# Sliding-window attention and gated convolution FFN: three V loads on ScalarE's DMA queue, with new order lists

## The chip, the core and the metric

The kernel runs on one core of a Trainium2 chip. The core has five engines that work side by side: TensorE (PE) for matmuls, VectorE (DVE), ScalarE (ACT) and GpSimd (POOL) for everything element by element, and SyncE (SP), which here only issues DMAs. ScalarE can issue DMAs too, on a queue of its own. Each engine runs its instructions strictly in order; between engines, semaphores make an instruction wait for what it needs. The metric is the device time of one execution in microseconds (us); the time of a kernel is the median of several runs.

## What is computed

For 8 sequences of 576 positions, 8 heads of 64: attention in which position i sees only positions within 32 of it, then a gated FFN with a convolution of three taps along the sequence.

```
scores = (q @ k^T) / 8, only where |i - j| <= 32
x      = softmax(scores) @ v          # heads side by side: 512 wide
h      = relu(x @ w_in)               # 512 -> 1024
c[s]   = w0*h[s-1] + w1*h[s] + w2*h[s+1]   # per channel
out    = (h * sigmoid(c)) @ w_out     # 1024 -> 512
```

Inputs and output are float32; the kernel computes matmuls in bf16.

## The kernel before

**Attention** is done by sequence b (0 to 7) and half s (0 or 1). For each half, `load_qk` (L502) loads q and k in two pieces each, one for heads 0 to 3 and one for heads 4 to 7, 288 KB a piece, in runs of 2304 bytes. `load_v` (L534) loads V in chunks of 128 positions that are shifted by 32 (chunk 0 has 96 rows, chunk 4 has 96); its runs are 256 bytes, since a row of one head is 64 floats. For sequence 0, chunk 2 is split into rows 0 to 64, which belong to half 0, and rows 64 to 128, which belong to half 1. `cast_qk` (L514) turns q and k to bf16; `cast_v` (L544) makes the bf16 tile ve of V, and `shift_v` (L553) a second one, vo, which holds V shifted by 64 positions. `transposes` (L591) brings q and k to head-dimension-major form through PE, and a copy from PSUM by ACT or DVE writes qT or kT. `scores` (L635) multiplies them and takes exp on ACT (L683); the window is kept either by a matmul that adds a band of large negative numbers, or by a multiplication with a mask on POOL or DVE (L690). `values` (L693) multiplies with V on PE (L711), takes the reciprocal of the sums (L729) and writes the normalised rows xn on DVE (L731). `turn` (L738) transposes xn into xT: with PE for sequences 0 and 1, and by a DMA transpose on SP's queue (L744) for the others.

**The FFN** works on 12 chunks of 384 positions; chunks 0 and 1 are cut into two pieces each. For each of 8 blocks m of 128 hidden channels, `hidden` (L811) multiplies with w_in (L856), takes relu on ACT into hT (L876), applies the three taps in one of five ways (PE with diagonal matrices L931, ACT L939, DVE L944, or all three taps on POOL, L919 and L924), takes tanh on ACT (L954; the gate is written with tanh), and gates on DVE (L971). `project` (L985) multiplies with w_out (L996), copies from PSUM to y, and stores (L1014, the last chunk L1010).

**Weights.** w_in and w_out come in two halves of 1 MB each through the same two staging tiles wst (L576) and are cast block by block; w_in's casts may be on ACT, POOL or DVE, w_out's are on POOL. The 24 diagonal matrices of the taps (L489 on ACT, L491 on DVE) are made from `conv_w`, which ACT's queue loads (L475) and PE transposes (L478).

**Order.** Each of these steps is an operation with a number. Nothing is planned while the program is built: `ORDER` lists all operation numbers in program order, `PICK` names the engine for those that have a choice, `CHOICE` the way in which each block's taps or each window mask is done, `BANKS` the PSUM bank for each use. `Plan.place` walks through ORDER and gives each operation a start by its own cost figures; the start only sorts the operations of all engines into one program and says where `warm` puts idle matmuls (L1023) that keep PE busy in the head. So within one engine or queue, program order is the order of these lists. Every load but conv_w is on SP's queue. A load into a staging tile waits there until its former content has been cast, and all that stands behind it in the queue waits too.

Of the kernel before, what the change touches and what calls it, by code (L numbers as in the profile page):

```python
# [17 lines left out]
    0, 0, 0, 0, 1, 0, 0, 2, 0, 0, 4, 4, 4, 4, 3, 2, 4, 4, 4, 4, 0, 4, 4, 4, 2, 4, 0, 2, 0, 0, 0, 4,  # L18
    4, 4, 4, 4, 4, 4, 4, 4, 4, 4, 0, 4, 2, 1, 1, 2, 2, 0, 2, 0, 2, 4, 3, 4, 4, 2, 2, 2, 1, 2, 1, 2,
    3, 0, 3, 2, 2, 2, 2, 2, 0, 2, 2, 3, 0, 1, 2, 2, 4, 0, 0, 2, 1, 2, 4, 2, 2, 2, 2, 3, 2, 3, 2, 0,  # L20
    2, 0, 2, 2, 2, 2, 1, 1, 0, 2, 2, 3, 2, 1, 4, 2, 2, 0, 3, 2, 2, 0, 2, 0, 2, 2, 2, 2, 4, 3, 3, 2,
    3, 3, 2, 2, 2, 2, 2, 2, 2, 2, 2, 3, 2, 2, 3, 3, 2, 2, 3, 2, 3, 2, 3, 2,
# [11 lines left out]
    67, 74, 0, 29, 36, 30, 27, 34, 37, 51, 1, 47, 2, 22, 12, 21, 48, 52, 28, 35, 45, 49, 50, 46, 55,  # L34
    53, 26, 25, 7, 68, 75, 89, 85, 86, 4, 56, 32, 33, 70, 69, 43, 76, 77, 44, 91, 87, 18, 54, 8, 31,
    42, 24, 38, 92, 14, 11, 88, 72, 83, 41, 39, 57, 58, 5, 60, 61, 90, 95, 59, 62, 63, 64, 65, 66,
    97, 17, 96, 82, 93, 117, 121, 225, 98, 120, 99, 118, 219, 119, 221, 223, 112, 114, 213, 6, 94,
    226, 113, 16, 211, 116, 40, 115, 71, 81, 217, 215, 78, 79, 220, 222, 73, 224, 80, 84, 100, 214,
    212, 103, 251, 216, 13, 133, 140, 9, 3, 19, 218, 227, 132, 139, 236, 101, 10, 23, 252, 102, 104,
    105, 233, 228, 229, 110, 106, 20, 108, 253, 243, 107, 111, 152, 148, 230, 109, 262, 244, 245,  # L40
    246, 153, 247, 15, 231, 232, 237, 263, 382, 234, 383, 384, 239, 240, 135, 134, 142, 141, 150,
    385, 238, 241, 388, 154, 151, 248, 149, 242, 155, 249, 250, 235, 258, 259, 268, 264, 265, 269,
    389, 158, 159, 171, 177, 156, 157, 256, 254, 386, 387, 376, 276, 378, 255, 260, 377, 286, 257,
    277, 402, 374, 379, 287, 288, 261, 278, 403, 283, 380, 170, 176, 136, 172, 178, 122, 125, 126,
    123, 143, 270, 279, 173, 179, 396, 375, 381, 271, 124, 137, 280, 294, 404, 397, 284, 272, 398,
    188, 190, 266, 186, 184, 285, 295, 296, 393, 411, 281, 191, 282, 273, 185, 394, 189, 187, 395,
    274, 405, 406, 267, 407, 412, 390, 399, 275, 400, 408, 391, 413, 401, 392, 409, 197, 198, 146,
    410, 138, 144, 147, 127, 130, 195, 163, 160, 161, 162, 164, 131, 196, 192, 193, 129, 128, 461,
    462, 306, 307, 312, 165, 166, 168, 169, 305, 304, 311, 320, 321, 174, 145, 318, 319, 194, 297,
    298, 289, 290, 322, 167, 418, 414, 415, 323, 324, 416, 291, 325, 426, 422, 182, 342, 341, 180,  # L50
    346, 353, 357, 417, 433, 420, 175, 183, 292, 423, 427, 293, 354, 358, 419, 181, 436, 421, 437,
    328, 438, 434, 435, 202, 308, 313, 339, 340, 345, 329, 326, 199, 351, 203, 204, 439, 327, 355,
    430, 352, 440, 200, 201, 431, 441, 442, 432, 330, 301, 302, 309, 316, 356, 363, 364, 359, 360,
    310, 317, 314, 331, 332, 334, 209, 210, 428, 429, 361, 333, 335, 336, 451, 456, 207, 452, 453,
    424, 315, 468, 343, 349, 469, 475, 443, 205, 362, 299, 425, 486, 457, 446, 447, 448, 458, 471,
    470, 476, 344, 348, 454, 206, 455, 208, 487, 459, 449, 488, 489, 444, 544, 545, 482, 540, 541,
    484, 485, 300, 445, 450, 350, 347, 368, 460, 483, 365, 366, 369, 370, 367, 506, 507, 511, 522,
    523, 493, 494, 504, 505, 510, 546, 547, 518, 519, 520, 516, 542, 543, 568, 556, 521, 517, 564,
    569, 490, 491, 473, 478, 557, 570, 526, 527, 558, 492, 495, 565, 566, 567, 463, 464, 559, 560,
    550, 551, 548, 549, 528, 554, 555, 529, 530, 472, 480, 474, 477, 481, 499, 500, 496, 497, 501,  # L60
    524, 552, 656, 657, 663, 371, 338, 508, 514, 512, 571, 584, 525, 498, 585, 586, 561, 674, 553,
    572, 562, 573, 563, 574, 575, 587, 588, 509, 579, 580, 576, 581, 670, 671, 465, 466, 692, 337,
    372, 596, 597, 675, 479, 513, 515, 531, 532, 534, 535, 533, 582, 577, 583, 536, 598, 599, 602,
    603, 608, 617, 627, 600, 604, 578, 628, 618, 695, 694, 699, 706, 693, 658, 698, 659, 664, 609,
    708, 709, 610, 601, 622, 605, 707, 611, 672, 673, 589, 619, 629, 623, 620, 621, 630, 631, 644,
    645, 624, 710, 711, 640, 641, 632, 633, 676, 677, 606, 607, 642, 612, 591, 636, 788, 373, 613,
    614, 660, 303, 590, 625, 615, 704, 592, 705, 643, 646, 647, 616, 637, 638, 626, 593, 594, 648,
    634, 635, 639, 715, 716, 503, 789, 795, 502, 729, 730, 661, 666, 790, 737, 738, 802, 803, 806,
    807, 681, 745, 718, 682, 763, 719, 741, 742, 733, 734, 678, 679, 764, 746, 765, 683, 717, 680,
    668, 665, 747, 766, 767, 712, 735, 773, 697, 791, 796, 804, 649, 713, 736, 805, 662, 669, 687,  # L70
    688, 774, 689, 739, 684, 685, 686, 539, 537, 467, 650, 740, 768, 769, 748, 749, 538, 696, 870,
    871, 731, 755, 756, 757, 732, 743, 750, 759, 653, 775, 776, 744, 760, 770, 667, 771, 864, 751,
    777, 702, 758, 772, 752, 654, 703, 793, 792, 778, 860, 865, 808, 884, 861, 885, 761, 714, 762,
    809, 753, 754, 779, 651, 652, 700, 701, 720, 899, 800, 812, 798, 797, 866, 862, 813, 721, 780,
    886, 887, 722, 888, 723, 983, 794, 801, 817, 724, 867, 863, 872, 818, 725, 879, 819, 880, 980,
    981, 987, 873, 889, 890, 874, 875, 868, 869, 894, 876, 810, 811, 900, 827, 831, 881, 895, 882,
    903, 896, 897, 877, 691, 690, 824, 982, 823, 883, 904, 785, 783, 595, 786, 891, 892, 784, 905,
    906, 901, 878, 893, 898, 907, 908, 909, 988, 781, 782, 910, 1000, 1001, 814, 815, 816, 994, 995,
    996, 997, 822, 727, 828, 726, 919, 998, 902, 999, 911, 920, 921, 922, 834, 835, 935, 936, 1005,
    1002, 826, 830, 825, 829, 940, 838, 839, 1006, 1003, 931, 932, 937, 938, 836, 925, 941, 837,  # L80
    939, 832, 926, 840, 923, 927, 841, 942, 943, 929, 924, 949, 848, 928, 950, 944, 945, 946, 845,
    912, 930, 849, 799, 958, 951, 952, 846, 1112, 985, 990, 933, 842, 914, 833, 1016, 850, 1111,
    1017, 655, 728, 1018, 821, 959, 913, 947, 948, 953, 954, 843, 934, 963, 915, 968, 1007, 820,
    1057, 1118, 1129, 1130, 844, 1022, 1059, 955, 956, 960, 961, 964, 1053, 1054, 1060, 1058, 969,
    965, 966, 1004, 916, 917, 1125, 1065, 847, 984, 992, 851, 970, 962, 971, 967, 957, 986, 993,
    989, 1008, 1066, 1032, 1126, 1083, 1033, 972, 1084, 852, 1009, 853, 1055, 1056, 1078, 1019,
    1023, 1034, 1113, 787, 1021, 1035, 1069, 1070, 1073, 1028, 1029, 1010, 1085, 1079, 1080, 1011,
    1081, 1030, 1031, 1012, 1013, 1074, 1082, 1075, 973, 974, 1071, 1072, 1025, 1063, 1064, 1038,
    854, 855, 1061, 1076, 1077, 856, 1091, 1092, 1093, 1062, 1039, 1086, 1087, 975, 976, 991, 1094,
    1114, 1020, 1026, 1115, 1041, 1042, 1119, 1127, 1131, 1132, 1128, 1088, 1089, 1120, 1043, 1040,  # L90
    977, 978, 1136, 1137, 1133, 1067, 1096, 1068, 1036, 1116, 1027, 1121, 1024, 1123, 1090, 1095,
    1138, 1097, 1047, 1048, 1049, 1134, 1037, 1135, 1147, 1148, 1153, 1149, 1163, 1150, 1154, 1100,
    1098, 1099, 1164, 857, 859, 858, 1183, 1189, 1190, 1184, 1044, 1045, 1214, 1193, 1194, 1191,
    1192, 1159, 1160, 1165, 1195, 1196, 1161, 1162, 1046, 1215, 1166, 1216, 1117, 1124, 1142, 1143,
    1144, 1152, 1156, 1101, 1102, 1222, 1103, 1217, 1218, 1223, 1226, 1139, 1140, 1141, 1185, 1187,
    1186, 1204, 1205, 1199, 1188, 1197, 1198, 1104, 1209, 1015, 918, 1014, 1105, 1200, 1206, 1210,
    1224, 1211, 1225, 1122, 1050, 1051, 1244, 1245, 1227, 1230, 1207, 1219, 1248, 1212, 1231, 1232,
    1220, 1249, 1221, 1233, 1108, 1109, 1201, 1202, 1213, 1203, 1234, 1106, 1169, 1271, 1228, 1229,
# [206 lines left out]
def kernel(  # L305
# [84 lines left out]
    def pe(n, count=1):  # L390
        return ("PE", count * (n / 2400.0 + 0.003))
# [708 lines left out]
```

## Time and profile before

| | |
|---|---|
| median of 7 runs | 220.13 us (219.85 to 220.47) |
| the profiled execution | 219.31 us |
| its span (first to last instruction) | 217.6 us |
| TensorE clock granted | 0.997 |
| busy: PE, DVE, ACT, POOL | 199.0, 194.0, 189.0, 180.3 us |
| DMA traffic | 45.92 MB, nearly all on one queue |

The span is what the profile shows; the profiled execution's own time is 1.71 us longer. In the profile's rows a line number is a line of the kernel; L400, L402 and L406 are the helper `copy` on ACT, POOL and DVE, so that one has to read the names of the tiles: st for q and k as loaded (qst, kst), nat as cast (qn, kn), vst, ve, vo, wst. "SPq" and "ACTq" are the issues of DMAs. In brackets stands how long the engine had been idle and what ended it.

### The profile page before, as it was taken

How to read it: one execution, taken by the hardware profiler on the slowest of the kernel's cores; microseconds unless marked ns; L12 is line 12 of the kernel's file. 1: busy time of each engine (PE TensorE's matmuls, PEld its weight loads, DVE VectorE, ACT ScalarE, POOL GpSimd, SP SyncE). 2: the span in 40 equal slices, each digit the busy share in tenths (PEclk: the TensorE clock that was granted, in tenths of full speed). 3: DMA queues.
4: the chain of work that ended last, by engine and by line, in shares of the span. 5: the costliest groups of instructions: out<-in, count | busy, mean ns of one | idle time of the engine just before them, and what ended most of it. 6: DMA issues, size and time to landing. Idle time of an engine off the chain costs nothing.

```text
span 217.6 us, 6442 instructions
## 1 busy us (share of the span) xinstructions
PE 199.0 (91%) x2445; PEld 124.8 (57%) x2462; DVE 194.0 (89%) x391; ACT 189.0 (87%) x406; POOL 180.3 (83%) x225
## 2 busy tenths in 40 slices
PE   2577789998999989999999999999999999999993
PEld 0454668967777566656555475456566455455441
DVE  5468996769899899999999999999999999999962
ACT  3198999976798999999998999799999999999860
POOL 3352999999886866999999999999999999999940
PEclk9999999999999999999999999999999999999998
DMA  5999999998993599999899999998399531170074
GB/s 170 261 275 347 333 326 274 350 266 182 314 232 98 78 222 306 220 282 229 165 216 270 212 293 262 285 257 228 84 137 217 110 145 26 39 275 18 0 281 154
DMA packets 68675, 45.92 MB, mean 211 GB/s; under 512 B 53644, under 2 KB 53924, under 8 KB 68644
## 3 DMA queue, kind: packets, MB, share of 16 engines
q1 hardware_dynamic: 68608, 45.49, 83.8%
q8 instruction: 19, 0.31, 0.7%
q14 instruction: 12, 0.10, 0.2%
q10 hardware_dynamic: 36, 0.01, 0.0%
HBM read 32.52 MB, written 9.44 MB: 193 GB/s over the span
## 4 chain that ended last, share of the span: by engine, by line
POOL 39%; PE 25%; DVE 14%; ACT 7%; DMA 7%; issue 5%; SPq 1%; POOLq 1%; DVEq 0%
POOL tmp L924 13%; POOL tmp L919 12%; PE ps_all L996 8%; PE ps_all L856 6%; POOL vo L402 6%; POOL ve L402 4%; PE ps_all L608 3%; DMA xT<-xn 2%; DMA vst<-in_v_dram 2%; POOL kn L402 2%; DMA kst<-in_k_dram 2%; DVE xn L731 2%; ACT ps_all L954 2%; PE ps_all L931 2%; ACT attn L683 2%
## 5 line engine op out<-in xcount | busy, mean ns | idle before, releaser
L856 PE MATMUL ps_all<-xT,w_in_sb 128*128 128x385 bf16 (+4 forms) x448 | 73.6, 305 | 2.4 <-DVE w_in_sb L406 1.3
L944 DVE SCALAR_TENSOR_TENSOR ps_all<-hT,conv_w_sb,ps_all 128x384 f32<-128x384 bf16 (+3 forms) x117 | 65.6, 594 | 3.7 <-PE ps_all L931 2.0
L996 PE MATMUL ps_all<-w_out_sb,gT 128*128 128x512 bf16 (+1 forms) x279 | 66.1, 373 | 2.0 <-DVE y L406 0.5
L971 DVE SCALAR_TENSOR_TENSOR gT<-ps_all,hT 128x384 bf16<-128x384 f32 (+3 forms) x112 | 51.5, 492 | 3.5 <-ACT ps_all L954 2.9
L856 PEld LDWEIGHTS <-w_in_sb 128*128 128x128 bf16 x448 | 40.0, 98 | 23.7 <-issue 2.5
L876 ACT ACTIVATE hT<-ps_all 128x385 bf16<-128x385 f32 (+4 forms) x112 | 48.5, 466 | 3.6 <-PE ps_all L856 3.3
L996 PEld LDWEIGHTS <-gT 128*128 128x128 bf16 x296 | 28.1, 98 | 31.0 <-issue 1.8
L683 ACT ACTIVATE attn<-ps_all 128x1024 bf16<-128x1024 f32 (+1 forms) x40 | 37.1, 951 | 3.4 <-PE ps_all L668 3.3
L924 POOL TENSOR_TENSOR tmp<-tmp 128x384 f32<-128x384 f32 (+1 forms) x38 | 37.3, 982 | 3.2
L954 ACT ACTIVATE ps_all<-ps_all 128x384 f32<-128x384 f32 (+3 forms) x93 | 38.6, 449 | 0.2
L402 POOL TENSOR_SCALAR vo<-vst 64x1024 bf16<-64x1024 f32 (+1 forms) x32 | 33.3, 1041 | 6.1 <-DMA vst<-in_v_dram 3.7
L919 POOL TENSOR_SCALAR tmp<-hT,conv_w_sb 128x384 f32<-128x384 bf16 (+1 forms) x57 | 34.4, 610 | 3.8 <-ACT hT L876 2.1
L939 ACT ACTIVATE ps_all<-hT,conv_w_sb 128x384 f32<-128x384 bf16 (+3 forms) x49 | 28.2, 582 | 2.5 <-DVE gT L971 1.8
L731 DVE TENSOR_TENSOR xn<-ps_all,rec 128x512 bf16<-128x512 f32 (+1 forms) x32 | 25.6, 817 | 0.5
L402 POOL TENSOR_SCALAR ve<-vst 128x512 bf16<-128x512 f32 (+1 forms) x38 | 24.3, 648 | 1.4
L402 POOL TENSOR_SCALAR qn<-qst 128x1152 bf16<-128x1152 f32 (+1 forms) x19 | 19.2, 1017 | 6.6 <-DMA qst<-in_q_dram 5.8
L400 ACT COPY y<-ps_all 128x512 f32<-128x512 f32 (+1 forms) x28 | 16.3, 590 | 5.3 <-PE ps_all L996 5.3
L402 POOL TENSOR_SCALAR kn<-kst 128x1152 bf16<-128x1152 f32 (+1 forms) x17 | 17.6, 1036 | 2.8 <-DMA kst<-in_k_dram 2.7
L608 PE MATMUL ps_all<-ident,kn 128*128 128x128 bf16 x144 | 13.1, 224 | 6.0 <-DVE kn L406 5.9
L931 PE MATMUL ps_all<-hT,diag_w 128*128 128x192 bf16 (+3 forms) x113 | 17.1, 271 | 0.0
L711 PE MATMUL ps_all<-ve,attn 128*64 128x65 bf16 x384 | 15.2, 197 | 1.5 <-DVE ve L406 0.6
L400 ACT COPY kT<-ps_all 128x640 bf16<-128x640 bf16 (+1 forms) x21 | 15.7, 755 | 0.9 <-PE ps_all L668 0.7
(66 smaller groups left out, 238.4 us busy)
## 6 DMA issues: line engine op xcount, KB each, us to landing
qst<-in_q_dram SPq DMA_DIRECT2D x32, 288.0 KB, 5.4
kst<-in_k_dram SPq DMA_DIRECT2D x32, 288.0 KB, 5.8
out_dram<-y SPq DMA_DIRECT2D x11, 768.0 KB, 5.7
vst<-in_v_dram SPq DMA_DIRECT2D x23, 256.0 KB, 5.0
vst<-in_v_dram SPq DMA_DIRECT2D x16, 192.0 KB, 5.3
wst<-in_moe_w_in_dram SPq DMA_DIRECT2D x2, 1024.0 KB, 8.8
wst<-in_moe_w_out_dram SPq DMA_DIRECT2D x2, 1024.0 KB, 8.2
out_dram<-y SPq DMA_DIRECT2D x2, 256.0 KB, 2.0
```

What stands on the lines that cost most here:

```text
L400: nc.scalar.copy(out=out_, in_=in_)
L402: nc.gpsimd.tensor_scalar(out=out_, in0=in_, scalar1=1.0, scalar2=0.0, op0=ALU.mult, op1=ALU.add)
L683: add(act(2 * w), t + 0.1, lambda e: nc.scalar.activation(at, ps(sl, 0, 1024).rearrange("p (e x) -> p e x", e=2)[:, :, 0:w], AF.Exp, bias= ...
L731: add(dve(4 * n * D), t + 0.1, lambda e: nc.vector.tensor_tensor(out=xn[i].rearrange("p c (e g) d -> p (c e) g d", e=2)[:, 2 * cs[0]:2 * ( ...
L856: nc.tensor.matmul(ps(sl, 512 * y, 512 * y + n), w_in_sb[:, kc, m * 128:(m + 1) * 128], x_[:, kc, a0:a1], start=(kc == 0), stop=(kc == KC ...
L876: nc.scalar.activation(o_, i_, AF.Relu, bias=0.0, scale=0.5)
L919: nc.gpsimd.tensor_scalar(out=tv(not own), in0=hview(m, o0, o1, kk - 1), scalar1=conv_w_sb[:, kk, m:m + 1], scalar2=0.0, op0=ALU.mult, op1 ...
L924: nc.gpsimd.tensor_tensor(out=tv(0), in0=tv(0), in1=tv(1), op=ALU.add)
L944: add("DVE", tt + 0.1, lambda e, m=m, y=y, n_=n_, pv=pv, ks=by_dve: nc.vector.scalar_tensor_tensor(out=pv(y), in0=hview(m, o0, o1, ks[n_] ...
L954: nc.scalar.activation(o_, i_, AF.Tanh, bias=0.0, scale=1.0)
L971: nc.vector.scalar_tensor_tensor(out=o_, in0=i_, scalar=1.0, in1=hview(m0, o0, o1, 0, w), op0=ALU.add, op1=ALU.mult,)
L996: nc.tensor.matmul(ps(sl, f0, f1), gT[ig][:, m, 128 * i:128 * i + 128], w_out_sb[:, m, f0:f1], start=(m == 0), stop=(m == MB - 1),)
```

## The change

Three loads of V for sequence 0, half 0 (chunk 0, chunk 1, and rows 0 to 64 of chunk 2: 192, 256 and 128 KB) are issued by ScalarE instead of SyncE:

```diff
+    def queue(second):
+        return (("ACTQ", 0.6), nc.scalar) if second else (sp(), nc.sync)
...
     def load_v(b, c, p0, p1, prio, rel):
         s0 = 128 * c - PAD + p0
-        add(sp(0.57), prio, lambda e: nc.sync.dma_start(
+        on, q_ = queue(b == 0 and p0 < 64 and c < 3)
+        add(on, prio, lambda e: q_.dma_start(
             vst[p0:p1, c, :, :], v[b, :, s0:s0 + p1 - p0, :].rearrange("h p d -> p h d")
...
-        on = dict([act(n), pool(n), both(n)]) if b == 0 else pool(n)
+        on = dict([act(n), pool(n), ("DVE", n / 960.0 + 0.14)]) if b == 0 else pool(n)
```

The last pair is in `cast_qk` and, like the other numbers that the diff changes in `load_qk`, `load_v`, `load_w` and `conv_weights` (cost figures and a mode), it only feeds the figures of `Plan.place`. `CHOICE`, `ORDER`, `PICK` and `BANKS` are new in whole. Read as lists by engine, these are the differences that the prediction speaks of:

| | before | after |
|---|---|---|
| SP's queue, first issues | q half 1 (1 piece), k half 0 (2), q half 0 (2), q half 1 (1), V chunk 1, V chunk 2 rows 0 to 64, k half 1 (2), V chunk 0, V chunk 3, w_in (2), V chunk 2 rows 64 to 128, V chunk 4, then sequence 1 | k half 0 (2), q half 0 (2), q half 1 (1), k half 1 (2), q half 1 (1), w_in (2), V chunk 4, V chunk 2 rows 64 to 128, V chunk 3, then sequence 1 |
| ACT's queue | conv_w | conv_w, V chunks 0, 1, 2 rows 0 to 64 |
| PE, first | k transposes, conv_w between them, q, scores | conv_w, k transposes, q, scores |
| DVE, first | q cast, k cast, conv_w copy, 2 diagonals, kT copy, qT copy | conv_w copy, 4 diagonals, V casts 0 and 1, a V shift, 2 kT copies, qT copy |
| PE, half 0 of sequence 0 | scores, half 1's transposes, both values | scores, values, transposes, values, transposes |
| first w_in block used (7) is cast by | DVE, behind 2 xT copies | POOL |
| SP's queue, transposes of sequence 2 | two, then V of sequence 3 (chunks 3, 4) and a q load, two more, then the k loads of sequence 4 | four, with V's chunk 3 ahead, and chunk 4 and the k loads behind |

| operations | before | after |
|---|---|---|
| q/k casts on ACT, DVE, POOL | 1, 3, 36 | 2, 1, 37 |
| V casts on ACT, DVE, POOL | 2, 1, 38 | 0, 2, 39 |
| V shifts on ACT, DVE, POOL | 1, 3, 32 | 1, 5, 30 |
| w_in and w_out casts on ACT, DVE, POOL | 2, 4, 10 | 2, 3, 11 |
| diagonals on ACT, DVE | 15, 9 | 11, 13 |
| y copies on ACT, DVE | 28, 9 | 30, 7 |
| window by band, POOL mask, DVE mask | 20, 4, 16 | 19, 5, 16 |
| blocks with all taps on POOL | 19 | 19 |

## The prediction

> **What bounds the kernel now.** I read the page's chain first, then busy time by stage, then the first 23 us in order of time, then the DMA view.
>
> ```profile
> POOL 39%; PE 25%; DVE 14%; ACT 7%; DMA 7%; issue 5%; SPq 1%; POOLq 1%; DVEq 0%
> ```
>
> No engine owns the end; the chain changes hands. Stage by stage (columns: length, then busy us of PE, PEld, DVE, ACT, POOL, granted clock, DMA share, GB/s):
>
> ```profile
> 0.00:22.80 22.80, 13.11 (x176) 8.20 (x176) 14.92 (x44) 13.54 (x25) 9.05 (x21) 1.00 0.96 262
> 22.80:46.00 23.20, 21.97 (x368) 19.03 (x370) 19.13 (x46) 21.78 (x66) 22.18 (x33) 1.00 1.07 316
> 66.90:99.00 32.10, 31.36 (x430) 19.64 (x432) 31.02 (x59) 30.80 (x62) 26.78 (x33) 1.00 1.01 198
> 99.00:140.00 41.00, 40.39 (x467) 23.40 (x470) 40.22 (x73) 38.36 (x75) 39.20 (x41) 1.00 1.02 238
> ```
>
> From 22.8 us on all four engines are nearly full (in 99 to 140: DVE idle 0.8 of 41, POOL 1.8). Only the head is loose: PE idles 9.7 of 22.8 us, DVE 7.9, POOL 13.8, while the DMA engines are 96% busy. The head is bound by data, the rest by total work. A change of load order can win in the head; afterwards only moved work or changed stalls count.
>
> The first 23 us in order of time (start, length, ..., idle before and its releaser):
>
> ```profile
> 8.96 0.67 POOL L402 TENSOR_SCALAR qn<-qst 128x576 bf16<-128x576 f32 x1 [0.53 <-DMA qst<-in_q_dram]
> 11.66 0.62 POOL L402 TENSOR_SCALAR vo<-vst 64x512 bf16<-64x512 f32 x1 [1.09 <-DMA vst<-in_v_dram]
> 14.03 1.02 ACT L683 ACTIVATE attn<-ps_all 128x1024 bf16<-128x1024 f32 x1
> 15.07 0.62 POOL L402 TENSOR_SCALAR vo<-vst 64x512 bf16<-64x512 f32 x1 [0.51 <-DMA vst<-in_v_dram]
> 17.08 0.19 PE L711 MATMUL ps_all<-ve,attn 128*64 128x65 bf16 x1 [0.60 <-DVE ve L406]
> 18.59 0.62 POOL L402 TENSOR_SCALAR w_in_sb<-wst 128x512 bf16<-128x512 f32 x1 [1.94 <-DMA wst<-in_moe_w_in_dram]
> 22.83 3.67 PE L856 MATMUL ps_all<-xT,w_in_sb 128*128 128x256 bf16 x32 [1.33 <-DVE w_in_sb L406]
> ```
>
> The second half of q of half sequence 0 landed at 8.96, V's chunk 1 at 11.66, V's chunk 0 at 15.07, the first half of w_in at 18.59. The second exp was done at 15.05, but the rest of P times V went at 17.08: V's late chunks and their casts cost 2.0 us. The first hidden matmul (L856) starts at 22.83. V is slow to move: from 12 to 15.2 us mostly V, from 15.2 to 16.5 w_in:
>
> ```profile
> DMA packets 1957, 0.77 MB, mean 240 GB/s; under 512 B 1811, under 2 KB 1811, under 8 KB 1957
> DMA packets 256, 0.51 MB, mean 393 GB/s; under 512 B 7, under 2 KB 7, under 8 KB 256
> ```
>
> **Part 1, three V issues go to ScalarE's queue.** They take 192, 256 and 128 KB off SP's queue. SP's issue rows are 0.65 us each and V's chunk 1, issued at 4.71, landed 7 us later, so SP's issue time wasn't the limit: leaving SP is worth 0 by itself, what counts is the order. On ACT they cost 3 x 0.60 (the row of the one ACT issue) = 1.8 us: 0.8 to 3.2 with the conv issue, then the table load (1.28) to 4.5. ACT's first work before began at 4.75 after 2.04 of idle: hidden; without that cover, 1.8. If the issue of V waits for the zeroing of the V tile (DVE, 1.62 to 2.73), it starts up to 1.3 late, behind it only the other V issues, the table load and ACT's first scalings.
>
> Here the Trainium skill speaks against the change: "DMA: Bandwidth & Descriptors", section "Issuing engines are not separate DMA queues", says that issues from several engines run on the same 16 DMA engines and interleave, so only the initiation time is saved. The row: 96% DMA busy already with one queue. By the rule q pays for V's bytes; without it q would land at 8.96 as before and the first hidden matmul about 1.0 earlier than I reckon. I follow the rule. By then 1152 KB of q and k and 576 KB of V must have come: six q/k transfers, the same 1728 KB, had landed by 9.9; V's 0.59 MB at 220 to 240 instead of 270 GB/s adds 0.4. So the last of q is at **10.3** (bounds: 9.0 if q keeps its rate, 12.5 if the mix runs at the 170 GB/s of the page's first slice).
>
> **Part 2, the chain of the first half.** q at 10.3 instead of 8.96 is 1.3 late; its two casts now run on ACT and POOL side by side instead of one after the other on POOL, -0.3: scores, exps **1.0 late**, second exp done at 16.05. V has long landed, so its 2.0 us wait goes: P times V at 16.1 to 16.5, reciprocal 0.2, xn 0.65 (group 2 is normalised before, behind the first exp): xn done at 17.5 instead of 19.77. Then, on DVE, a qT copy 0.82, xT 0.65, a w_in cast 0.8, xT 0.65: 20.4. Before it was two xT and a w_in cast, 3.06 with gaps. With 0.6 for the matmul's own wait L856 starts at **21.0 instead of 22.83: -1.8**. On DVE the V casts and one shift (0.6 + 0.6 + 0.7) now stand in front of the two kT copies: if V's chunk 2 is late, kT is late.
>
> **Part 3, w_in ahead of the second half's V.** 256 KB less of V lies before it; at 240 GB/s that is 1.1: w_in lands at 17.5, its second half 1.1 earlier as well. Chunks 3, 4 and the rest of 2 land behind w_in, with the same 5.5 MB in all as before; ACT cast chunk 4 at 25.07 without waiting, so that they are hidden behind the first hidden chunk, with some 2 us of cover; beyond that each us is one for the second half's P times V.
>
> So the lead at 23 us is between 1.1 (w_in's second half, the later data) and 1.8; I carry **-1.5**.
>
> **Part 4, the new lists.** Counting the operations that the lists put on each engine, and pricing differences with their rows: *ACT* four diagonal scalings less (-1.4), two V casts less (-1.2), two y copies more (+1.2), two 384-wide L939 less and four narrow ones for one (-0.1), copies +0.4: -1.1. *DVE* two q/k casts less (-1.5), a w_in cast less (-0.8), two y copies less (-1.4), two wide and two 255-wide taps less for two narrow (-1.4), four diagonals more (+1.4), one V cast and two shifts more (+1.9), the rest +0.7: -1.1. *PE* tap matmuls +0.8, mask adds -0.1: +0.7. *POOL* a q/k cast, a V cast and a w_in cast more (+2.0), a 512-wide mask more (+1.15), two shifts less (-1.2), a tap block of 129 for one of 255 (-0.9): +1.0. From 99 us on the chain is POOL's, but POOL idles 5.3 us in 66.9 to 99, so most is covered; uncovered it is 1.0. I take **+0.3**. The tail keeps its shape (0).
>
> A stall that could move: SP's queue at the transposes of sequence 2.
>
> ```profile
> 70.41 2.60 SPq L744 DMA_TRANSPOSE xT<-xn  x2
> 73.11 2.13 SPq L536 DMA_DIRECT2D vst<-in_v_dram  x2
> 75.33 0.57 SPq L505 DMA_DIRECT2D qst<-in_q_dram  x1
> 75.97 2.58 SPq L744 DMA_TRANSPOSE xT<-xn  x2
> ```
>
> Two transposes held SP for 6.1 us (its longest wait), and loads of V and k queue behind them; POOL then idles 1.8 and 1.2 for them. In the new order four transposes stand together, with V's chunk 4 and the k loads of sequence 4 behind. Bounds: -3 (POOL's 5.3 idle shrinks) to +3 (k lands after POOL asks for it, near 80 us); value 0, since V's chunk 3 of sequence 3, for which POOL waited 1.8, now goes out ahead of the group, while the k loads now go behind two more transposes.
>
> **Sum.** 219.31 (span 217.60 and 1.71 around it) - 1.5 + 0.3 = 218.1 in the profile's terms; the median of the runs is 0.82 above the profiled one, so **218.9**.
>
> **The rivals.**
> *A, the lead is lost by 99 us.* For: the same bytes in all, POOL without idle from 21 to 65, and POOL sets the second half. Against: PE and DVE carried the chain from 20 to 66, and POOL waited 2.1 us at 66.9 for hT. Time: no lead left, the added POOL work covered by its idle time: 220.1.
> *B, slower: the first half's q, or V's chunk 2 ahead of kT on DVE, comes too late.* The page's section "Queues, rings and completion order" has each DMA engine take whole packets from its queues in turn; no row here has two busy queues. q and k move in runs of 2304 bytes, V in runs of 256, so turns could share time in a way that holds V back. For: 240 GB/s where V moves, and DVE runs in order. Against: V needs only a third of the bytes. It decides at 10.3 + 1.8 = 12.1 us: a landing later than that takes the whole gain. At 13.5 it is +1.4, with +0.3 of work less what overlaps: 221.2.
> *C, the stall at the transposes shrinks too* by about 2 of its 3: 216.9.
>
> **Numbers.** Likeliest case 0.45, its own range 218.0 to 219.6; A 0.17; B 0.20; C 0.18. A change within 0.2% (0.44 us) is about what a measurement of this kernel can't tell from none. Faster: 0.43 + 0.18 + 0.05 of A = 0.66. Same: 0.09 of A and 0.01 = 0.10. Slower: 0.20 + 0.03 + 0.01 = 0.24. The range leaves out the outer part of B and of C: 216.5 to 221.3.
>
> **What would show it.** V's casts of half 0 on DVE before 9 us; the second q cast near 10.4; no wait of L711 for V; first L856 at 21.0; first w_in cast at 17.5; POOL's taps (L919, 66.90 before) about 1.2 earlier; POOL busy near 181. Wrong: a DVE wait for V with kT behind it; L856 at or after 22.8; the gap in POOL near 80 us longer than 3.

## The result and the profile after

| | before | after |
|---|---|---|
| median of the runs | 220.14 us (31 runs, 218.71 to 221.59) | 218.38 us (12 runs, 217.17 to 218.91) |
| ratio, 95% interval | | 0.9903 (0.9881 to 0.9926) |
| profiled execution, its span | 219.31, 217.6 | 217.17, 215.1 |
| busy: PE, DVE, ACT, POOL | 199.0, 194.0, 189.0, 180.3 | 199.1, 188.1, 189.4, 181.6 |

The changed kernel is 1.0% faster by the ratio, which is taken over all runs; the medians are 1.76 us apart. 218.9 was forecast. Ratios and medians leave out an execution over 1.5% above the fastest of its kernel, of which this study has one (224.89 us, in the second experiment).

Lines of the code are 5 to 7 further down from the loads on: L863 is the hidden matmul (L856 before), L690 the exp, L718 P times V, L738 the write of xn, L926 POOL's taps, L751 the DMA transposes; `copy` is L401 on ACT, L403 on POOL, L407 on DVE. The experiments' kernels are numbered 0 or 11 further than that; the one built on the old lists is numbered 0 or 1 further than the kernel before.

The chain that ended last, by engine, of the changed kernel:

```profile
PE 54%; POOL 14%; DVE 14%; ACT 9%; DMA 5%; issue 3%; POOLq 0%; DVEq 0%; ACTq 0%
```

POOL's share has gone from 39% to 14%, PE's from 25% to 54%. That needs no new bound: all engines are nearly full behind the head (the rows below), so a small shift can move the chain from one to another. Busy time by stage of the changed kernel (length, then busy us of PE, PEld, DVE, ACT, POOL, granted clock, DMA share, GB/s):

```profile
0.00:22.80 22.80, 15.96 (x201) 10.34 (x202) 15.26 (x50) 14.18 (x26) 11.39 (x24) 1.00 1.00 293
22.80:46.00 23.20, 21.67 (x365) 17.73 (x364) 18.49 (x47) 20.35 (x62) 19.48 (x31) 1.00 1.04 309
...
66.90:99.00 32.10, 31.74 (x399) 19.64 (x401) 30.73 (x56) 31.32 (x63) 29.08 (x34) 1.00 1.01 208
99.00:140.00 41.00, 40.74 (x441) 23.58 (x444) 39.35 (x77) 40.14 (x83) 38.96 (x43) 1.00 1.00 240
```

The difference is in the first row: in the same 22.8 us PE works 2.85 us more (1.04 of it idle matmuls) and POOL 2.3 more, and data come at 293 instead of 262 GB/s. The head of the changed kernel in order of time (start, length, ..., idle before and its releaser):

```profile
7.57 0.43 DVE L407 CAST ve<-vst 128x512 bf16<-128x512 f32 x1 [1.60 <-DMA vst<-in_v_dram]
8.43 3.40 PE L1030 MATMUL ps_all<-ones,ident 128*128 128x384 bf16 x12
9.83 0.67 POOL L403 TENSOR_SCALAR qn<-qst 128x576 bf16<-128x576 f32 x1 [1.35 <-DMA qst<-in_q_dram]
11.12 0.42 DVE L407 CAST vo<-vst 64x512 bf16<-64x512 f32 x1 [3.12 <-DMA vst<-in_v_dram]
11.58 1.43 DVE L407 COPY kT<-ps_all 128x512 bf16<-128x512 bf16 x2
11.67 0.67 PE L615 MATMUL ps_all<-ident,qn 128*128 128x128 bf16 x9
13.69 0.41 PE L675 MATMUL ps_all<-qT,kT 64*128 64x64 bf16 x16 [0.71 <-DVE qT L407]
14.15 1.94 ACT L690 ACTIVATE attn<-ps_all 128x1024 bf16<-128x1024 f32 x2 [0.96 <-PE ps_all L675]
15.23 0.22 PE L718 MATMUL ps_all<-ve,attn 128*64 128x65 bf16 x1 [0.41 <-ACT attn L690]
15.55 0.62 POOL L403 TENSOR_SCALAR w_in_sb<-wst 128x512 bf16<-128x512 f32 x1 [1.80 <-DMA wst<-in_moe_w_in_dram]
16.96 0.69 DVE L738 TENSOR_TENSOR xn<-ps_all,rec 128x512 bf16<-128x512 f32 x1
19.30 0.68 DVE L407 CAST xT<-ps_all 128x512 bf16<-128x512 f32 x1
20.14 0.60 PE L863 MATMUL ps_all<-xT,w_in_sb 128*128 128x256 bf16 x4
```

V's two casts on DVE are done by 8.0 us, the last q of half 0 landed at 9.83, the second exp was done at 16.09 and xn at 17.65; P times V goes without any wait for V. The first hidden matmul starts at 20.14 instead of 22.83. Two waits are new. DVE stood 3.12 us, until 11.12, for V's chunk 2 (the shift into vo), with the two kT copies behind it. And PE was in 12 idle matmuls until 11.8, so that the q transposes began at 11.67, though the last q cast was done at 10.5. The first w_in block was ready for its cast at 15.55, 3.0 us earlier than before.

SP's queue at the transposes of sequence 2, in order of time, changed kernel:

```profile
65.27 8.17 SPq L751 DMA_TRANSPOSE xT<-xn  x4
73.48 0.58 SPq L542 DMA_DIRECT2D vst<-in_v_dram  x1
74.11 2.51 SPq L510 DMA_DIRECT2D kst<-in_k_dram  x4
```

And POOL's casts that need those loads:

```profile
81.92 1.15 POOL L403 TENSOR_SCALAR kn<-kst 128x1152 bf16<-128x1152 f32 x1 [1.02 <-DMA kst<-in_k_dram]
83.53 1.15 POOL L403 TENSOR_SCALAR qn<-qst 128x1152 bf16<-128x1152 f32 x1 [0.46 <-DMA qst<-in_q_dram]
```

Four transposes held SP for 8.2 us, and POOL waited 1.0 and 0.5 us for the k and q behind them; before it idled 1.8 for V and 1.2 for k.

### The profile page after: what moved, and what is told of

It reads as the page before. It is cut to its first block, busy times and chain, and to the rows that moved or that the text cites. A ratio compares the mean times of both kernels' runs of the same rounds, so it can differ in the third digit from the quotient of the medians.

```text
span 215.1 us, 6466 instructions
## 1 busy us (share of the span) xinstructions
PE 199.1 (93%) x2445; PEld 125.3 (58%) x2464; DVE 188.1 (87%) x392; ACT 189.4 (88%) x403; POOL 181.6 (84%) x227
## 4 chain that ended last, share of the span: by engine, by line
PE 54%; POOL 14%; DVE 14%; ACT 9%; DMA 5%; issue 3%; POOLq 0%; DVEq 0%; ACTq 0%
PE ps_all L1003 19%; PE ps_all L863 17%; POOL tmp L931 5%; PE ps_all L718 5%; POOL tmp L926 5%; PE ps_all L615 4%; PE ps_all L938 4%; DMA vst<-in_v_dram 4%; PE ps_all L675 3%; ACT attn L690 2%; POOL vo L403 2%; DVE xn L738 2%; ACT ps_all L961 2%; DVE qT L407 2%; ACT hT L883 2%
## 5 line engine op out<-in xcount | busy, mean ns | idle before, releaser
L863 PE MATMUL ps_all<-xT,w_in_sb 128*128 128x385 bf16 (+4 forms) x448 | 73.6, 305 | 2.4 <-ACT hT L883 1.4
L951 DVE SCALAR_TENSOR_TENSOR ps_all<-hT,conv_w_sb,ps_all 128x384 f32<-128x384 bf16 (+2 forms) x115 | 64.1, 592 | 1.7 <-ACT ps_all L946 0.9
L863 PEld LDWEIGHTS <-w_in_sb 128*128 128x128 bf16 x448 | 39.9, 98 | 22.6 <-issue 2.8
L883 ACT ACTIVATE hT<-ps_all 128x385 bf16<-128x385 f32 (+4 forms) x112 | 47.7, 453 | 3.1 <-PE ps_all L863 2.0
L961 ACT ACTIVATE ps_all<-ps_all 128x384 f32<-128x384 f32 (+3 forms) x93 | 39.5, 442 | 1.9 <-PE ps_all L938 1.2
L690 ACT ACTIVATE attn<-ps_all 128x1024 bf16<-128x1024 f32 (+1 forms) x40 | 36.9, 950 | 1.8 <-PE ps_all L675 1.4
L926 POOL TENSOR_SCALAR tmp<-hT,conv_w_sb 128x384 f32<-128x384 bf16 (+1 forms) x57 | 34.3, 609 | 4.9 <-ACT hT L883 3.0
L403 POOL TENSOR_SCALAR vo<-vst 64x1024 bf16<-64x1024 f32 (+1 forms) x30 | 32.2, 1075 | 4.9 <-DMA vst<-in_v_dram 2.4
L946 ACT ACTIVATE ps_all<-hT,conv_w_sb 128x384 f32<-128x384 bf16 (+2 forms) x50 | 28.1, 571 | 0.4
L403 POOL TENSOR_SCALAR ve<-vst 128x512 bf16<-128x512 f32 (+1 forms) x39 | 25.8, 668 | 1.6 <-DMA vst<-in_v_dram 0.3
L738 DVE TENSOR_TENSOR xn<-ps_all,rec 128x512 bf16<-128x512 f32 (+1 forms) x32 | 25.6, 814 | 0.4
L401 ACT COPY y<-ps_all 128x512 f32<-128x512 f32 (+1 forms) x30 | 17.6, 596 | 4.0 <-PE ps_all L1003 3.9
L403 POOL TENSOR_SCALAR kn<-kst 128x1152 bf16<-128x1152 f32 (+1 forms) x18 | 18.4, 1021 | 3.2 <-DMA kst<-in_k_dram 2.8
L403 POOL TENSOR_SCALAR qn<-qst 128x1152 bf16<-128x1152 f32 (+1 forms) x19 | 18.6, 980 | 2.6 <-DMA qst<-in_q_dram 2.2
L938 PE MATMUL ps_all<-hT,diag_w 128*128 128x384 bf16 (+3 forms) x114 | 18.1, 275 | 0.4 <-ACT attn L690 0.2
L718 PEld LDWEIGHTS <-attn 128*64 128x64 bf16 x640 | 12.5, 111 | 6.9 <-issue 2.3
L401 ACT COPY qT<-ps_all 128x640 bf16<-128x640 bf16 (+1 forms) x18 | 13.5, 752 | 3.2 <-PE ps_all L615 3.1
L718 PE MATMUL ps_all<-ve,attn 128*64 128x65 bf16 x384 | 15.2, 197 | 0.9 <-ACT attn L690 0.4
```

What stands on the lines that cost most here:

```text
L401: nc.scalar.copy(out=out_, in_=in_)
L403: nc.gpsimd.tensor_scalar(out=out_, in0=in_, scalar1=1.0, scalar2=0.0, op0=ALU.mult, op1=ALU.add)
L690: add(act(2 * w), t + 0.1, lambda e: nc.scalar.activation(at, ps(sl, 0, 1024).rearrange("p (e x) -> p e x", e=2)[:, :, 0:w], AF.Exp, bias= ...
L718: nc.tensor.matmul(ps(sl, lo, lo + D + 1, 64 * j, 64 * j + 64), attn[a][:, 512 * h_ + col:512 * h_ + col + 64], (vo if tt % 2 else ve)[i][ ...
L863: nc.tensor.matmul(ps(sl, 512 * y, 512 * y + n), w_in_sb[:, kc, m * 128:(m + 1) * 128], x_[:, kc, a0:a1], start=(kc == 0), stop=(kc == KC ...
L883: nc.scalar.activation(o_, i_, AF.Relu, bias=0.0, scale=0.5)
```

## The experiments

Each run has its own runs of the kernel before beside it (medians 220.26 to 220.34), so ratios are compared. Where two ratios are set against each other, the interval of the difference is put together from the two as if they were independent.

**One queue: is ACT's queue needed?** The changed kernel with V back on SP. The list order puts V there between the pieces of k and q.

```diff
-        on, q_ = queue(b == 0 and p0 < 64 and c < 3)
+        on, q_ = queue(False)
```

> The kernel after, with the three V loads back on SyncE's queue, interleaved with the k and q loads where the new order list has them (k, V chunk 0, k, V chunk 1, q, V chunk 2, q); all else is the same. If the load order makes the gain and the second queue none: 218.2 to 218.8 us, the first w_in cast at about 15.6, the first L863 at 20.1 as in the kernel after. If the second queue itself moves more bytes (293 GB/s in the first 22.8 us after, 262 before): the rate falls back towards 262, the first w_in cast to 16.8 or later, the first L863 to 21.2 or later, and the time to 219.3 or more.

Measured: 218.05 us, ratio 0.9896 (0.9859 to 0.9932), the same as with two queues. From the timeline of this one-queue kernel:

```profile
9.60 0.42 DVE L407 CAST vo<-vst 64x512 bf16<-64x512 f32 x1 [1.41 <-DMA vst<-in_v_dram]
10.36 0.67 POOL L403 TENSOR_SCALAR qn<-qst 128x576 bf16<-128x576 f32 x1 [1.70 <-DMA qst<-in_q_dram]
19.98 0.60 PE L863 MATMUL ps_all<-xT,w_in_sb 128*128 128x256 bf16 x4
```

Its first stage, with the columns of the stages above:

```profile
0.00:22.80 22.80, 16.44 (x202) 10.51 (x203) 15.63 (x50) 14.22 (x26) 11.33 (x24) 1.00 0.98 281
```

V's chunk 2 is whole 1.5 us earlier than with two queues and q 0.5 later: the same bytes in another sequence, and the first hidden matmul comes at nearly the same time. The rate, 281 GB/s, lies between the 293 with two queues and the 262 before, without a cost in time. So the gain is that of the new lists and not of the second queue. The lists change the order of the loads, PE's order in half 0 and the engine that casts the first w_in block all at once; what each of these is worth was not tried apart.

**The queue alone: the kernel before with only V's three loads on ACT's queue**, all lists as before.

```diff
-        add(sp(0.57), prio, lambda e: nc.sync.dma_start(
+        on, q_ = (("ACTQ", 0.6), nc.scalar) if b == 0 and p0 < 64 and c < 3 else (sp(0.57), nc.sync)
+        add(on, prio, lambda e: q_.dma_start(
```

> The kernel before with its own lists, with only the three V loads on ScalarE's queue. If order alone counts, V lands early but q and k of half 0 pay for it; P times V no longer waits for V, w_in lands no earlier: 219.7 to 220.6. If the second queue itself moves more bytes, w_in lands at 17.5 or earlier instead of 18.6 and the time is 219.0 to 219.6.

Measured: 221.92 us, ratio 1.0069 (1.0037 to 1.0100): slower than before, outside both expectations. The timeline of this kernel (L684 is the exp, L609 the transposes, L712 P times V):

```profile
10.05 0.67 POOL L402 TENSOR_SCALAR qn<-qst 128x576 bf16<-128x576 f32 x1 [7.29 <-DMA qst<-in_q_dram]
11.38 1.35 POOL L402 TENSOR_SCALAR qn<-qst 128x576 bf16<-128x576 f32 x2 [0.66 <-DMA qst<-in_q_dram]
16.32 1.01 ACT L684 ACTIVATE attn<-ps_all 128x1024 bf16<-128x1024 f32 x1
18.28 0.66 PE L609 MATMUL ps_all<-ident,kn 128*128 128x128 bf16 x9 [1.18 <-DVE kn L406]
18.79 0.42 DVE L406 CAST ve<-vst 128x512 bf16<-128x512 f32 x1
22.47 1.29 DVE L406 CAST xT<-ps_all 128x512 bf16<-128x512 f32 x2 [0.51 <-PE ps_all L754]
25.03 2.14 PE L857 MATMUL ps_all<-xT,w_in_sb 128*128 128x256 bf16 x18 [1.34 <-DVE w_in_sb L406]
```

With V on a second queue, and half 1's first q piece still ahead of everything on SP, the last q of half 0 is there at 11.38 instead of 8.96. POOL shifts V from 12.8 on without waiting for it, and yet P times V did not go at 17.33, when the second exp was done: in the old lists half 1's transposes on PE (18.28) and DVE's cast of V (18.79) stand ahead of it, so most of it runs from 19.27 on. So xT comes at 22.5 and the first hidden matmul 2.2 later than before. V early is paid for by q; without the rest of the change that is a loss.

**Is the lead of the head kept to the end?** In the changed kernel, the copy of xT for chunk 0 of sequence 0 (DVE, 0.69 us) is done five times.

```diff
-        add(dict([act(KC * cols), dve(KC * cols)]), t + 0.1, lambda e: copy(
-            e, o_, ...
-        ), reads
+        add(dict([act(KC * cols), dve(KC * cols)]), t + 0.1, lambda e: [copy(
+            e, o_, ...
+        ) for _ in range(5 if (b, c) == (0, 0) else 1)], reads
```

> The kernel after, with the copy of xT chunk 0 of sequence 0 on VectorE done five times instead of once: four copies of 0.69 are a delay of 2.75 us, the whole lead of the first L863 (22.83 before, 20.14 after). If the lead at the head is what reaches the end: 220.2 to 221.2, that is all of the gain lost. If the head's lead is lost on the way and the new lists win later: below 219.0.

Measured: 221.14 us, ratio 1.0033 (1.0015 to 1.0052). The timeline of this kernel:

```profile
20.16 3.58 DVE L407 CAST xT<-ps_all 128x512 bf16<-128x512 f32 x5
23.89 2.98 PE L863 MATMUL ps_all<-xT,w_in_sb 128*128 128x256 bf16 x24 [3.03 <-DVE xT L407]
```

And its second stage (columns as above, granted clock third from the end):

```profile
22.80:46.00 23.20, 20.45 (x317) 17.33 (x318) 18.75 (x44) 18.00 (x57) 16.27 (x26) 1.00 0.93 282
```

The row has grown from 0.68 to 3.58 us, by 2.9; the median is 2.76 above the changed kernel's. PE's wait of 3.03 us could have cost something of its own, its clock: 19 of the 22 executions have a mean granted clock of 0.983 to 0.992, where all 12 of the changed kernel have 0.997 or more. But the three executions at 1.000, the profiled one among them, took 220.36, 220.94 and 221.16 us, still 2.0 to 2.8 above the changed kernel's median. What the head loses arrives at the end nearly in full.

**Is w_in ahead of V's chunk 3 worth anything?** Chunk 3 (256 KB) goes back ahead of w_in on SP.

```diff
 SP's queue in ORDER, first half of sequence 0:
-  ..., q half 1, w_in, w_in, V chunk 4, V chunk 2 rows 64 to 128, V chunk 3
+  ..., q half 1, V chunk 3, w_in, w_in, V chunk 4, V chunk 2 rows 64 to 128
```

> The kernel after, with V chunk 3 of sequence 0 ahead of w_in in SyncE's queue, as before the change (256 KB). By the prediction's third part w_in lands 1.1 later, and the time is 219.0 to 219.5. If the first L863 is bound by xT (written until 19.98) and w_in (first cast at 15.55) has room, w_in is later by 0.7 to 1.1 but the time stays within 0.3 of the kernel after: 218.1 to 218.7.

Measured: 218.41 us, ratio 0.9905 (0.9878 to 0.9931): no difference. The timeline of this kernel:

```profile
16.95 0.62 POOL L414 TENSOR_SCALAR w_in_sb<-wst 128x512 bf16<-128x512 f32 x1 [2.87 <-DMA wst<-in_moe_w_in_dram]
19.54 0.69 DVE L418 CAST xT<-ps_all 128x512 bf16<-128x512 f32 x1
20.37 0.60 PE L874 MATMUL ps_all<-xT,w_in_sb 128*128 128x256 bf16 x4
```

w_in lands 1.4 us later, and the first hidden matmul still waits for xT, which is done at 20.23. w_in had that much room.

**The two new waits of the head, one by one and together.** First, the V shift that DVE waits with goes behind the kT and qT copies:

```diff
 DVE's part of ORDER:
-  V cast, V cast, V shift, kT copy, kT copy, qT copy
+  V cast, V cast, kT copy, kT copy, qT copy, V shift
```

> The changed kernel with one operation moved in the list: VectorE's shift of V, which waited until 11.1 us for the late V chunk 2, goes behind the two kT copies and the qT copy. Theory 1 (the V wait in front of the copies sets the head, and a lead in the head is carried whole): scores 0.7 to 1.0 us earlier, first hidden matmul near 19.3, median 217.4 to 217.8. Theory 2 (the 12 idle matmuls ahead of the q transposes on TensorE set the head): first hidden matmul stays at 20.1 and the median at 218.4.

Second, half as many idle matmuls in the head, in `warm`:

```diff
                 more.append((t + 0.05, spin))
-                t += 0.5
+                t += 1.0
```

> The changed kernel with half as many idle matmuls in the head and nothing else. If VectorE's wait for V's chunk 2 sets the head: first hidden matmul at 20.1, median 218.2 to 218.6. If the idle matmuls do: first hidden matmul 0.5 to 1.0 earlier, median 217.4 to 217.9. If each hides the other, only both together gain, and this one alone stays at 218.2 to 218.6.

Third, both ("the run before" is the one with the moved shift):

> As the run before, and half as many idle matmuls in the head, so that the q transposes need not wait for them. Theory 1 (V wait): nothing more than with the moved shift alone, 217.4 to 217.8. Theory 2 (idle matmuls): first hidden matmul 0.7 to 1.0 earlier than in the changed kernel, median 217.4 to 217.8, with the moved shift alone at 218.4. If both are needed or the lead gets lost later: 218.2 to 218.6 here.

| | median | ratio to before | first hidden matmul in its profile |
|---|---|---|---|
| the change | 218.38 | 0.9903 (0.9881 to 0.9926) | 20.14 |
| shift moved | 217.51 | 0.9876 (0.9853 to 0.9899) | 19.67 |
| half the idle matmuls | 218.61 | 0.9931 (0.9910 to 0.9952) | 22.47 |
| both | 216.66 | 0.9854 (0.9830 to 0.9878) | 19.14 |

The timeline of the kernel with the shift moved:

```profile
11.78 0.67 PE L626 MATMUL ps_all<-ident,qn 128*128 128x128 bf16 x9
```

The timeline of the kernel with both:

```profile
10.22 0.67 POOL L414 TENSOR_SCALAR qn<-qst 128x576 bf16<-128x576 f32 x1
10.95 0.68 PE L626 MATMUL ps_all<-ident,qn 128*128 128x128 bf16 x9 [0.40 <-POOL qn L414]
12.45 0.41 PE L686 MATMUL ps_all<-qT,kT 64*128 64x64 bf16 x16 [0.34 <-DVE qT L418]
```

Here the last cast of q began 0.4 later than in the changed kernel (10.22), and the scores still start 1.2 earlier (12.45). This version is faster than the change by 0.0049 (0.0016 to 0.0082) of the ratio, that is by 1.1 us; its median, 216.66, is below all that was expected of it, and it is the best version of this study.

The traces show how one wait hid the other. With the shift moved and all idle matmuls left, the q transposes still began at 11.78. The median, 217.51, is what the first theory expected, but the scores came only 0.4 earlier, and the gain in the ratio, 0.0027 (-0.0005 to 0.0059), is not resolved from none. Nor is the step from there to both, 0.0022 (-0.0011 to 0.0055): only the sum of the two steps is. Half the idle matmuls alone gain nothing, and in the profiled execution, which is 1.2 us above that kernel's median, they did harm. Its timeline:

```profile
11.75 0.72 DVE L407 CAST vo<-vst 64x512 bf16<-64x512 f32 x1 [4.05 <-DMA vst<-in_v_dram]
12.50 1.43 DVE L407 COPY kT<-ps_all 128x512 bf16<-128x512 bf16 x2
14.60 0.61 PE L675 MATMUL ps_all<-qT,kT 64*128 64x64 bf16 x16 [2.65 <-DVE qT L407]
```

And its busy time by stretch (columns as above, granted clock third from the end):

```profile
12.00:16.00 4.00, 1.40 (x35) 1.04 (x35) 3.97 (x9) 1.05 (x3) 2.15 (x4) 0.76 1.05 405
16.00:22.80 6.80, 6.67 (x112) 5.18 (x108) 4.93 (x11) 5.67 (x10) 2.33 (x4) 0.64 1.17 321
```

V's chunk 2 came late, DVE held the kT copies back, PE had nothing to do for 2.65 us, and after that its granted clock was 0.64 over 16 to 22.8 us, where the changed kernel had 1.00. The same 16 score matmuls took 0.61 instead of 0.41. "TensorE: Matmul & The Clock Gate" of the Trainium skill ("What's actually happening") gives an idle window of about 3.4 us for the clock to halve; here the clock fell after an unbroken wait of 2.65 us, while in the profile of the five xT copies it stayed at 1.00 after one of 3.03. So these runs give no fixed length.

The other executions agree. Of the 19 with half the idle matmuls, 12 have a mean granted clock of 0.984 to 0.992, with a median of 219.02 us; the other 7, at 0.996 or more, have 218.33, which is the changed kernel's time. (Where in the execution the clock fell is known of the profiled one alone, and 5 of the 24 executions of the kernel before beside it have such a clock too.) So without the clock's fall half the idle matmuls gain nothing alone, which fits DVE's wait taking it all, and with it they lose. The idle matmuls of the head are a cover for DVE's wait: they protect the clock while it is there, and are in the way once it is gone.

**Both, on one queue.** The diffs of both, and V on SP:

> As the run before, with V on SyncE's queue between the pieces of k and q, as in the one-queue run, where V's chunk 2 landed at 9.6 instead of 11.1 and the last q at 10.36 instead of 9.83. If q sets the head now: first hidden matmul 0.5 later than with two queues and the moved shift, median 0.3 to 0.6 more. If the second queue is worth nothing: the same within 0.3.

Measured: 217.42 us, ratio 0.9880 (0.9863 to 0.9898). The timeline of this kernel:

```profile
10.82 0.67 POOL L414 TENSOR_SCALAR qn<-qst 128x576 bf16<-128x576 f32 x1 [1.99 <-DMA qst<-in_q_dram]
13.51 0.61 PE L686 MATMUL ps_all<-qT,kT 64*128 64x64 bf16 x16
```

The last cast of q began 0.6 later than in the run with two queues, and the 16 score matmuls took 0.61 again after a wait, though the granted clock from 12 to 14 us reads 1.00. (In the kernel before, too, nine q transposes took 1.16 us at 10.16 and 0.68 at 13.13 with the clock's column at 1.00: it does not show every slow stretch of the head.) The difference in the ratio, 0.0026 (-0.0004 to 0.0056), points to the first expectation, but its interval includes none.

**Does q pay for V's bytes?** The version with both, with V on SP behind all four k and q pieces of half 0, and V's casts and shifts behind q's.

```diff
 SP's queue in ORDER (with queue(False)):
-  k, V chunk 0, k, V chunk 1, q, V chunk 2, q, half 1 of k and q, ...
+  k, k, q, q, V chunk 0, V chunk 1, V chunk 2, half 1 of k and q, ...
 ACT, DVE and POOL: V's casts and shifts behind the q casts and copies
```

> The kernel with the moved shift and half the idle matmuls, with everything on SyncE's queue and the three V loads behind the four k and q pieces of half 0 instead of among them; V's casts and shifts on VectorE, ScalarE and GpSimd go behind the q casts and copies. Theory 1 (q pays for V's bytes, and the head follows q): four pieces of 288 KB before q is whole, so the last q lands near 7.8, where the fourth piece landed in the kernel before, 2.4 earlier than with V beside it; the first hidden matmul moves from 19.1 to at most the time at which w_in and its casts allow it, 16.5 to 17.5; the time is that plus 197.0 to 198.0: median 214.2 to 215.8. Theory 2 (something else in the head, half 1's q and k or w_in, takes over): q near 7.8, but the first hidden matmul at 18.5 or later, median 216.0 to 217.0. Theory 3 (q does not pay for V's bytes): the last q at 9.5 or later, no gain.

Measured: 217.90 us, ratio 0.9886 (0.9853 to 0.9918): no better than the version it was made from (0.9854), and above the range of all its expectations that have q early. The timeline of this kernel:

```profile
7.82 0.67 POOL L414 TENSOR_SCALAR qn<-qst 128x576 bf16<-128x576 f32 x1 [3.03 <-DMA qst<-in_q_dram]
11.37 0.41 PE L686 MATMUL ps_all<-qT,kT 64*128 64x64 bf16 x16 [0.18 <-DVE qT L418]
14.03 0.67 POOL L414 TENSOR_SCALAR qn<-qst 128x576 bf16<-128x576 f32 x1 [0.32 <-DMA qst<-in_q_dram]
15.88 0.69 DVE L749 TENSOR_TENSOR xn<-ps_all,rec 128x512 bf16<-128x512 f32 x1
19.30 1.65 PE L874 MATMUL ps_all<-xT,w_in_sb 128*128 128x256 bf16 x12 [0.37 <-DVE xT L418]
```

q pays: without V beside it the last q is there at 7.8 instead of the changed kernel's 9.8. But for what follows the mechanism of the second expectation holds. The scores start at 11.37, and then the lead runs into half 1: its q lands at 14.03, its transposes stand on PE between the two multiplications with V, the second xn comes at 15.88, and the first hidden matmul is no earlier than in the version it was made from (19.14). Moving those transposes back was not tried.

**The rest of the stall at the transposes.** On SP, the last V piece of sequence 3 and the first two k loads of sequence 4 go ahead of the second of the four transposes.

```diff
 SP's queue in ORDER:
-  transpose, transpose, transpose, transpose, V chunk 4, k, k, k, k
+  transpose, V chunk 4, k, k, transpose, transpose, transpose, k, k
```

> The changed kernel with the last V piece of sequence 3 and the first two k loads of sequence 4 moved on SyncE's queue ahead of the second of the four transposes of sequence 2. Theory 1 (the rest of the stall at the transposes costs time, 3.0 us of GpSimd idle between 66.9 and 99): the gap of 1.0 near 82 goes, median 217.4 to 217.9. Theory 2 (GpSimd's idle time there costs nothing, since TensorE carries the chain): median 218.2 to 218.6. Theory 3 (the transposes then come late, and the FFN chunk behind them waits): above 218.8.

Measured: 218.14 us, ratio 0.9913 (0.9896 to 0.9930): no gain, next to the second expectation. The gap is gone (POOL, the same stretch), and nothing comes of it:

```profile
79.67 2.27 POOL L414 TENSOR_SCALAR kn<-kst 128x1152 bf16<-128x1152 f32 x2
81.91 1.15 POOL L414 TENSOR_SCALAR qn<-qst 128x1152 bf16<-128x1152 f32 x1
```

But over 66.9 to 99 us POOL still idles 2.7 us instead of 3.0: most of its idle time only went elsewhere.

## Why the prediction was right, point by point

The sign, the likeliest case and the outline of its mechanism were right: the new order wins in the head, and the rest of the kernel keeps what was won. One sum over all profiles shows that it is kept: the profiled time less the start of the first hidden matmul.

| kernel | time | first hidden matmul | rest |
|---|---|---|---|
| before | 219.31 | 22.83 | 196.48 |
| V on ACT's queue alone, old lists | 222.48 | 25.03 | 197.45 |
| the change | 217.17 | 20.14 | 197.03 |
| one queue | 216.97 | 19.98 | 196.99 |
| five xT copies | 221.16 | 23.89 | 197.27 |
| V chunk 3 ahead of w_in | 217.89 | 20.37 | 197.52 |
| shift moved | 216.75 | 19.67 | 197.08 |
| half the idle matmuls | 219.84 | 22.47 | 197.37 |
| both | 216.60 | 19.14 | 197.46 |
| both, one queue | 218.05 | 20.06 | 197.99 |
| q first | 217.16 | 19.30 | 197.86 |
| k ahead of transposes | 217.10 | 19.72 | 197.38 |

The start of the first hidden matmul varies by 5.9 us, the rest by 1.5. That the order of the loads alone makes the head shorter was not shown; PE's order may have a part in it (part 2).

- **Part 1.** That the second queue gains no time was right for the change (218.05 without it, 218.38 with it), and the Trainium skill's rule on which it rested agrees; in the version with both fixes it is open (217.42 without it, 216.66 with it). The landing of q, worked out from bytes, was 0.5 off: 10.3 forecast, 9.83 measured. That q pays for V was right too, but not what it pays: "without it q would land at 8.96 as before" forgot that 8.96 had a piece of half 1 ahead of it, which the new order moves back. Without V beside it q is there at 7.8, so V costs q 2.0 us.
- **Part 2.** Second exp 16.05 forecast, 16.09 measured; xn 17.5 and 17.65; no wait for V at P times V. That the exp agrees so well is luck, since the way there was another one: q came 0.5 earlier than forecast, and DVE's wait for V's chunk 2, named as a risk, and PE's idle matmuls, not seen at all, took it back. Nor were the 2.0 us before P times V all V's, as the prediction had it. A row of the kernel before:

```profile
15.47 0.66 PE L608 MATMUL ps_all<-ident,kn 128*128 128x128 bf16 x9 [1.18 <-DVE kn L406]
```

  The second exp was done at 15.05, and until 16.13 PE waited for k of half 1 and transposed it; only then came P times V and its waits for V. With V early and the old lists, 1.9 us still passed (17.33 to 19.27). The new lists move these transposes behind the first multiplication with V, so a part of the gain may be PE's order and not that of the loads. The step that failed is the last stretch, xn to the first hidden matmul: 2.9 us for DVE's copies and casts plus 0.6 for the matmul's own wait. Measured: 2.3 (the w_in cast in between was 0.42 instead of 0.8) and 0.16; the first block's w_in is POOL's to cast now, so that the matmul waits for xT alone. So L863 began at 20.14, 2.7 earlier than before instead of 1.8.
- **Part 3.** Wrong in size and in use. w_in landed 3.0 earlier, not 1.1, but xT sets the first hidden matmul: giving 1.4 of it back cost nothing (218.41). To carry -1.5 as a compromise between -1.1 and -1.8 was the mistake; the lead of 2.7 is carried nearly whole, as the five xT copies show for a delay.
- **Part 4.** +0.3 was small: the rest is 0.55 longer in the profile pair. With only one such profile of the kernel before, and 197.45 for the old lists in the other run, the price of the new lists is not settled within about 1 us (the rests of all other kernels are 197.0 to 198.0). By engine, PE, ACT and POOL came to +0.1, +0.4, +1.3 (forecast +0.7, -1.1, +1.0); DVE fell by 5.9 instead of 1.1, without showing in the rest.
- **Sum.** Profiled: -2.69 + 0.55 = -2.14, where -1.5 + 0.3 = -1.2 was forecast. The medians differ less, by 1.76: the changed kernel's profiled execution is 1.21 below its median, not 0.82 as assumed. So 218.9 became 218.38.
- **Rival A** (lead lost by 99 us) is out: 2.9 us of delay gave 2.76, and 2.0 to 2.8 in the executions at full clock. POOL's taps of the next chunk came 2.2 earlier (64.74 instead of 66.90), not the 1.2 forecast.
- **Rival B**'s mechanism was there: V's chunk 2 landed at 11.1, 1.0 short of the 12.1 that was named, with kT behind it. Together with the idle matmuls it cost 1.1 us of the gain, not all of it.
- **Rival C**: the stall did shrink (POOL's idle time in 66.9 to 99 from 5.3 to 3.0), but the two windows hold other work, 2 us apart; removing the remaining k and q gap changed nothing (218.14), and the rest of the kernel got no shorter, so nothing points to a part of the gain from it. That no such part exists is not shown. (The 6.1 us of the prediction were the longest wait of SP in that stretch; in the whole kernel it is 14.9.)

## What to carry to other kernels

In a head that is bound by data, do not count on a second queue: here it gained no resolved time. Write down for each piece when its consumer can first use it, and order the pieces by that, since a piece that goes early is paid for by those beside it: V cost q 2.0 us. Then look on each engine for a wait with needed work behind it in the list, whether for data or for work that could go later, and change two waits that hide each other together: alone, neither of the two here gave a resolved gain, together 1.1 us. Filler matmuls that protect the clock are part of that: they are needed while the wait is there and in the way when it is gone.

## What was not expected of the hardware

- V's chunk 2 (128 KB), issued on ACT's own queue by 3.2 us, landed at 11.1 us, 1.5 us later than when it was issued at 4.3 us on the same queue as k and q (9.6). A queue of its own made it later, not earlier (11.4 and 11.75 in two other kernels with two queues). How the transfers share the engines was not measured apart.
- PE's granted clock fell to about half after a single wait of 2.65 us in one profile, and stayed at 1.00 after one of 3.03 us in another.
- The same DVE instruction took different times in the two kernels: multiplications with the mask, 128x512, 1.28 us on average before (2) and 0.56 after (3); the diagonals 4.4 us for 9 before and 3.9 us for 13 after. The slowest mask, 2.14 us at 136.38 before, ran beside POOL's own multiplications with the mask (136.12 to 140.51); the other one before took 0.42. That POOL was the cause was not tried.
- The rate over the first 22.8 us rose from 262 GB/s to between 275 and 300 in all other kernels of the study. With the new lists it is 275 to 281 on one queue (three kernels) and 290 to 300 on two (seven); the old lists with two queues have 283. So two queues did move some more, without a resolved gain in time. What held the rate in the order before was not tried.
